# Sigmoid attention: the scores of four heads in one run, and their products with v in one run

## The chip, the cores and the metric

The kernel runs on one core of one Trainium2 chip. The metric is the device time of one execution, in microseconds (us). In the rows of the profile PE is TensorE (PEld its weight loads), ACT is ScalarE, DVE is VectorE, POOL is GpSimd and SP is SyncE, which issues the DMAs. A row of the timeline gives its start, its length, the engine, the line of the kernel, the operation, what it writes and reads, the shape, and how many instructions are merged in it; what stands in brackets is the time for which the engine was idle before it, and what ended that.

## What is computed

Attention with a sigmoid in place of the softmax, over 8 batches of 12 heads, 448 positions and 64 values a head, and then an MLP of 768 to 2048 to 768 with a sigmoid-approximated GELU over the 3584 tokens. All in float32.

```python
def _attn_ref(q, k, v):
    S = q.shape[2]
    scale = 1.0 / np.sqrt(q.shape[-1])
    scores = scale * np.matmul(q, k.transpose(0, 1, 3, 2)) - np.log(S)
    attn = 1.0 / (1.0 + np.exp(-scores))
    return np.matmul(attn, v).astype(np.float32)

def _moe_ref(x, w_in, w_out):
    h = x @ w_in
    g = h * (1.0 / (1.0 + np.exp(-1.702 * h)))
    return (g @ w_out).astype(np.float32)
```

Between the two, the heads of a position are put side by side into a row of x. The weights come as float64 words.

## The kernel before

**Pairs and chunks.** Two heads make a pair, 48 pairs in all; a pair's q and k, transposed, stand in one tile `qkraw` of 128 partitions (head 0 in 64 of them, head 1 in the other 64). The 448 keys are cut in three chunks of 128 and a left-over of 64. `split_pair` (line 541) splits q and k into a rounded part and a rest, both in a tile `qk`: the first on ACT or DVE (lines 442 and 443), the second on DVE (line 448). `scores` (line 567) makes the scores of one chunk for both heads in three terms, six matmuls; only the very first pair goes without a split. `scores_left` (line 585) makes the left-over scores of two pairs, four heads, at once, straight from `qkraw`. Each of these steps fills two banks of PSUM, and one `sigmoid` on ACT (line 560) empties them into an SBUF tile `a` (or `al` for the left-over). `values` (line 601) multiplies one chunk's `a` with v, and `values_left` (line 615) the left-over's; the products of both pairs of a unit of four heads are added up in one pair of banks, from which `to_x` (line 653) copies them into tiles of x, on ACT (line 658) or DVE (line 660), whichever the planner finds free. There are two copies per unit in the first and last batch, and four in the others, where a pair's rows fall in two blocks of x.

**Units.** Two pairs with one left-over are called a unit here: 24 of them. Before the change PE's order is: left-over scores of the unit; scores of its second pair; products of its first pair; scores of the next unit's first pair; products of this unit's second pair, with the left-over products at their end. So between a run of scores and the products that need its sigmoids another run always lies.

**Banks.** `two_banks` (line 555) gives the place numbers out: four pairs of banks, q0 to q3, place modulo 4. A step that writes a pair of banks waits for the readers of the step that had it before.

**The planner.** The kernel's instructions are put in order by a planner in the kernel's own text (`Plan.run`, line 106) before anything runs. PE's work comes as two lists of units, attention and MLP; a unit is begun when its tasks that are marked `alone` are ready, and is then issued whole, in its order. Work of ACT, DVE and SP goes by ready time and rank (`key`), the rank being that of the earliest PE step that needs it; `plan.early` sets the rank by hand for the copies to x and the loads of weights. On the chip each engine runs its list in that order and waits where it must. `BUFS` (line 27) tells how many tiles a ring has: a tile is written again when the readers of its last use are done.

**Beside attention.** The decoding of the weights from float64 (`decode`, line 460: sign, exponent and mantissa steps on DVE and ACT), the storing of decoded weights, and sums of weight blocks for the MLP run on DVE, ACT and SP while PE does attention. The MLP's first block (`first_block`, line 812) begins when the last attention unit is done; the other blocks follow in triples, with sums and differences of blocks in place of some products.

Of the kernel before, what the change touches and what calls it, by code (L numbers as in the profile page):

```python
# [24 lines left out]
WARM = 26  # L25

BUFS = dict(
    qk=2, vraw=3, a=5, al=1, raw64=2, e=4, qkraw=5, x32=8,
    pair=2, wsplit=4, q0=1, q1=1, q2=1, q3=1, h0=1, h1=1,
)  # L30
SLOTS = dict(s=1536, g=2048, t=384)
EARLY_SLOTS, LATE_SLOTS = dict(s=7, g=4, t=0), dict(s=0, g=9, t=13)
HORIZON, URGENT, SPARE, KEEP = 14, 4, 1, 2
AWAY = 3
AGAIN = ((1, 0), (1, 1))
BACKLOG, PRESSING = 6.0, 4

# [42 lines left out]
class Plan:  # L80
# [3 lines left out]
    def buffer(self, tag):  # L84
        b, ring = Buffer(), self.rings.setdefault(tag, [])
        b.turn = len(ring) % BUFS[tag]
        ring.append(b)
        return b
# [7 lines left out]
    def task(self, engine, cost, emit, deps=(), uses=()):  # L96
        return self.either({engine: cost}, {engine: emit}, deps, uses)
# [227 lines left out]
def sigmoid_attention_mlp(ctx: ExitStack, tc: tile.TileContext, qk, v, w, out):  # L325
# [11 lines left out]
    NC = S // P  # L337
# [38 lines left out]
    ps = spaces["q0"].tile([P, 512], F32, tag="q0_0", name="still", bufs=1)  # L376
# [9 lines left out]
    plan = Plan()  # L386
    task, either, buffer = plan.task, plan.either, plan.buffer
    def make(b, tag, shape, dtype, name):
        late = tag in LATE or tag == b.slot and int(tag[1:]) >= EARLY_SLOTS[tag[0]]
        if late and "late" not in spaces:  # L390
            att_stack.close()
            spaces["late"] = late_stack.enter_context(tc.tile_pool(name="late", bufs=2))
        if tag in ("h0", "h1") and tag not in spaces:
            for t in ("q1", "q0") if tag == "h0" else ("q3", "q2"):
                psum[t].close()
            banks(tag, "left" if tag == "h0" else "right")
        if late:
            pool = spaces["late"]
        else:
            pool = spaces.get(tag, sb)  # L400
        b.tile = pool.tile(shape, dtype, tag=tag if tag == b.slot else f"{tag}_{b.turn}", name=name, bufs=1)
        return b.tile
# [111 lines left out]
    x32, wrote, xs = {}, {}, {}  # L514
# [40 lines left out]
    def two_banks(place):  # L555
        b = buffer(f"q{place % 4}")
        b.tag = f"q{place % 4}"
        return b
# [8 lines left out]
    def scores(n, c, t_s, s, place):  # L567
        ps, a = two_banks(place), buffer("a")

        terms = ((0, 1), (1, 0), (0, 0)) if n else ((0, 0),)  # L570

        def emit():
            make(ps, ps.tag, [P, 2, 512], F32, f"sc{n}_{c}")
            src = [s.tile[:, 0], s.tile[:, 1]] if n else [s.tile]
            for i, (kk, qq) in enumerate(terms):
                for j, rows in enumerate(halves_of_rows):
                    nc.tensor.matmul(  # L577
                        ps.tile[:, j, :S], lhsT=src[kk][rows, S + c * P : S + (c + 1) * P], rhs=src[qq][rows, :S],
                        start=i == 0, stop=i == len(terms) - 1,
                    )  # L580

        t = task("PE", (0.7, 0.61, 0.61)[c] if n else 0.9, emit, t_s, [ps, s])
        return t, sigmoid(f"a{n}_{c}", a, ps, t), a

    def scores_left(n, sources, place):

        ps, a = two_banks(place), buffer("al")

        def emit():
            make(ps, ps.tag, [P, 2, 512], F32, f"sc{n}_{NC}")  # L590
            for cols, (_, src) in zip(halves_of_rows, sources):
                for j, rows in enumerate(halves_of_rows):
                    nc.tensor.matmul(  # L593
                        ps.tile[cols, j, :S], lhsT=src.tile[rows, S + NC * P :], rhs=src.tile[rows, :S],
                        start=True, stop=True, skip_group_check=True,
                    )

        t = task("PE", 0.8, emit, [t for ts, _ in sources for t in ts], [ps, *(b for _, b in sources)])
        return t, sigmoid(f"a{n}_{NC}", a, ps, t, "al"), a

    def values(n, c, t_a, a, t_v, vr, ps):

        def emit():
            if ps.tile is None:
                make(ps, ps.tag, [P, 2, 512], F32, f"av{n}")
            for j, cols in enumerate(halves_of_rows):
                at = ((n % 2 * 2 + j) * NC + c) * D
                nc.tensor.matmul(  # L608
                    ps.tile[cols, n % 2, :S], lhsT=vr.tile[:, at : at + D], rhs=a.tile[:, j],
                    start=c == 0, stop=False, skip_group_check=True,  # L610
                )

        return task("PE", (0.8, 0.75, 0.75)[c], emit, [t_a, t_v], [ps, a, vr])

    def values_left(t_a, a, t_v, vr, ps):

        def emit():
            for k, rows in enumerate(halves_of_rows):
                for j, cols in enumerate(halves_of_rows):
                    at = (4 * NC + j) * D  # L620
                    nc.tensor.matmul(  # L621
                        ps.tile[cols, k, :S], lhsT=vr.tile[rows, at : at + D], rhs=a.tile[rows, j],
                        start=False, stop=True, skip_group_check=True,
                    )

        return task("PE", 0.95, emit, [t_a, t_v], [ps, a, vr])
# [24 lines left out]
    copies = []  # L651

    def to_x(b, p, t, ps):
        bank = (b * NP + p) % 2
        for block, xb, first, into, cols in x32_places(b, p):
            n = cols.stop - cols.start
            copies.append(on_either(
                (0.2 + 0.00075 * n, lambda xb=xb, into=into, cols=cols: nc.scalar.copy(
                    xb.tile[:, into], ps.tile[:, bank, cols])),
                (0.15 + 0.00105 * n, lambda xb=xb, into=into, cols=cols: nc.vector.tensor_copy(  # L660
                    xb.tile[:, into], ps.tile[:, bank, cols])),
                [t], [xb, ps], first,
            ))
            wrote[block, p].append(copies[-1])
        split_x(b, p)
# [24 lines left out]
    firsts, urgent = [], []  # L690

    def attention():

        units, late, held_ = [], [], 0  # L700
        for n, (b, p) in enumerate(pairs):
            t_q, qkr, t_v, vr = load_pair(b, p)
            t_s, s = split_pair(b, p, t_q, qkr)
            firsts.append(t_s)
            left = scores_left(n, [first, (t_q, qkr)], held_ + 1) if n % 2 else None
            chunks = [scores(n, c, [t_s] if n else t_q[: c + 1], s, held_ + 1 + n % 2 + c) for c in range(NC)]
            run = [t for t, _, _ in chunks]
            if n % 2 == 0:
                first, chunks0, pair0 = (t_q, qkr), chunks, (b, p)
            else:  # L710

                units.append([left[0]])
                held_ += 1
                ps = two_banks(held_)
                both = [
                    [values(m, c, got[1], got[2], t_v, vr, ps) for c, got in enumerate(cs)]
                    for m, cs in ((n - 1, chunks0), (n, chunks))
                ]
                both[1].append(values_left(*left[1:], t_v, vr, ps))
                late.append(both[0])  # L720
                copied = len(copies)
                for pair in (pair0, (b, p)):
                    to_x(*pair, both[1][-1], ps)
                urgent.append(copies[copied:])
            if n > 2 and n % 2:

                plan.early += [(t, run[0]) for t in urgent[n // 2 - 1]]

            with_v = late.pop(0) if late else []
            for t in run[2:] + with_v:  # L730
                t.alone = False
            units.append(run + with_v)
            if n % 2:
                late.append(both[1])
        units.append(late.pop())
        place_of["next"] = held_ + 1
        return units

# [18 lines left out]
    def used_as(block):  # L757
        return [r for r, v in enumerate(W_USES) if v == block]
# [53 lines left out]
    def first_block():  # L812
# [5 lines left out]
        def pieces(m, h, i, got):  # L818
            out = []
            for k in range(2):  # L820
# [6 lines left out]
                count[0] += 1  # L827
                for r in used_as(2 * i + k) if (m, h) not in AGAIN else ():
                    save(m, r, h, slice(0, PIECE), into, b, t)
# [121 lines left out]
    def triple(one, blocks_before):  # L951
# [17 lines left out]
        def pieces_of(m, r):  # L969
            out = []  # L970
            for h in range(2):
                b, into, first = weights_ring(f"w{m}_{one}_{r}_{h}")
                ts = []
                if W_USES[r] < 8 and (m, h) in AGAIN:
                    i, k = divmod(W_USES[r], 2)
# [85 lines left out]
        class Net:  # L1061


            def __init__(self, m, defs, outs, uses, n, parts, name, finish):
# [18 lines left out]
                for v, cs in children.items():  # L1083
                    cs = sorted(cs, key=there)
                    for before, c in zip(cs, cs[1:]):
                        if c < len(PRODUCTS) and len(self.parents[c]) == 1:
                            away = there(c) - there(before)
                            if away >= AWAY:
                                self.seeds[c] = v
# [166 lines left out]
    main, nodes, ps = first_block()  # L1256
# [46 lines left out]
```

## Time and profile before

| what | time, us |
| --- | --- |
| median of 3 runs | 1060.55 (1060.08 to 1060.8) |
| the profiled execution | 1060.78 |
| its span, first to last instruction | 1059.0 |
| attention on PE, first scores to last left-over products | 3.93 to 261.2 |
| PE busy in the span | 1043.6 |
| DVE busy | 843.4 |
| ACT busy | 554.5 |
| longest wait of PE behind its warm-up (at 15.21, for DVE) | 2.00 |

The profiled execution lies 0.2 us over the median, and 1.8 us over its own span. Matmuls are pipelined, so their lengths overlap: how long a step holds PE is read from one start to the next, not from the length in the row. The granted clock of TensorE was 1.00 in all of the attention stage.

### The profile page before, as it was taken

To read this page: it belongs to the slowest core of one execution; us is meant where nothing else is said; L and a number is where in the kernel's file an instruction comes from. 1 tells how busy PE (TensorE), PEld (TensorE's weight loads), DVE (VectorE), ACT (ScalarE), POOL (GpSimd) and SP (SyncE) were. 2 spreads that over 40 slices of the span, in tenths; PEclk is the share of its full clock that TensorE was granted. 3 is DMA by queue.
4 is the path that set the end of the run, shared out by engine and by line. 5 is a ranking of instruction groups with operands and counts; after the bars stand their busy time and mean duration, and the time that the engine had idled before them with its cause. 6 is when DMAs were issued, how large, how long until landed. Compare 5 with 4: busy or idle time off the path is not lost.

```text
span 1059.0 us, 13676 instructions
## 1 busy us (share of the span) xinstructions
PE 1043.6 (99%) x5300; PEld 777.5 (73%) x5300; DVE 843.4 (80%) x770; ACT 554.5 (52%) x543; POOL 0.2 (0%) x4
## 2 busy tenths in 40 slices
PE   8999999999999999999999999999999999999997
PEld 4454545454788888888888788888888888788886
DVE  5988788873999856788898989999884596888684
ACT  7888788885655523434544444332443263534342
POOL 0000000000000000000000000000000000000000
PEclk9999999999999999999999999999999999999999
DMA  9899999883799997657656665869775545445765
GB/s 353 305 334 382 337 352 324 303 318 123 299 383 401 355 388 258 238 187 236 226 169 211 224 206 181 285 214 354 275 243 191 196 139 189 148 151 150 233 199 192
DMA packets 109104, 271.44 MB, mean 256 GB/s; under 512 B 8560, under 2 KB 69104, under 8 KB 106992
## 3 DMA queue, kind: packets, MB, share of 16 engines
q1 hardware_dynamic: 109040, 270.57, 73.1%
q8 instruction: 42, 0.69, 0.2%
q14 instruction: 22, 0.18, 0.1%
HBM read 185.60 MB, written 84.93 MB: 255 GB/s over the span
## 4 chain that ended last, share of the span: by engine, by line
PE 89%; DVE 4%; DMA 3%; ACT 2%; issue 1%; SPq 0%; ACTq 0%; DVEq 0%
PE p L800 54%; PE av L608 11%; PE sc L577 9%; PE h L800 6%; PE o_q L800 6%; PE av L621 2%; PE sc L593 2%; DMA qkraw<-qk 1%; DMA w<-c 1%; DMA w<-f 1%; DMA c<-wc 1%; DVE gp L1026 1%; ACT gp L1014 1%; DVE h L743 0%; ACT o L1156 0%
## 5 line engine op out<-in xcount | busy, mean ns | idle before, releaser
L800 PE MATMUL p<-gp,w 128*128 128x512 f32 x1440 | 329.5, 390 | 2.8 <-DVE gp L1026 1.2
L800 PE MATMUL p<-xp,w 128*128 128x512 f32 x1440 | 327.9, 389 | 1.0 <-DVE xp L1026 1.0
L800 PEld LDWEIGHTS p<-gp,w 128*128 128x128 f32 x1440 | 269.7, 188 | 61.3 <-DVE gp L1026 2.0
L800 PEld LDWEIGHTS p<-xp,w 128*128 128x128 f32 x1440 | 270.2, 188 | 57.5 <-DVE xp L1026 1.4
L563 ACT ACTIVATE a<-sc,bias 128x896 f32<-128x896 f32 x168 | 158.5, 1019 | 14.9 <-PE sc L577 10.9
L608 PE MATMUL av<-a,vraw 128*64 128x448 f32 x576 | 118.6, 547 | 0.0
L577 PEld LDWEIGHTS sc<-qk 64*128 64x128 f32 x846 | 75.8, 184 | 40.8 <-issue 14.0
L577 PE MATMUL sc<-qk 64*128 64x448 f32 x846 | 98.4, 373 | 2.6 <-DVE qk L448 2.0
L608 PEld LDWEIGHTS av<-a,vraw 128*64 128x64 f32 x576 | 37.1, 136 | 59.6 <-issue 56.4
L1026 DVE TENSOR_TENSOR gp<-h,gp 128x2048 fp32r<-128x2048 f32 x31 | 70.9, 2288 | 9.3 <-ACT gp L1014 8.9
L1156 ACT COPY h<-p 128x2048 f32<-128x2048 f32 x18 | 33.7, 1875 | 82.6 <-PE p L800 53.2
L800 PE MATMUL h<-x,w 128*128 128x512 f32 x288 | 66.6, 390 | 1.3 <-DVE x L660 1.3
L800 PE MATMUL o_q<-g,w 128*128 128x512 f32 x288 | 66.6, 389 | 1.2 <-ACT graw L856 1.2
L1190 DVE TENSOR_TENSOR h<-h,p 128x2048 f32<-128x2048 f32 x23 | 52.1, 2284 | 18.6 <-PE p L800 11.4
L1014 ACT CAST gp<-h 128x2048 fp32r<-128x2048 f32 x23 | 44.0, 1912 | 43.5 <-PE p L800 36.2
L800 PEld LDWEIGHTS h<-x,w 128*128 128x128 f32 x288 | 54.0, 188 | 13.3 <-DVE x L660 2.1
L800 PEld LDWEIGHTS o_q<-g,w 128*128 128x128 f32 x288 | 54.0, 188 | 12.8 <-ACT graw L856 1.6
L1156 ACT COPY o<-p 128x1536 f32<-128x1536 f32 x18 | 25.9, 1443 | 59.3 <-PE p L800 19.2
L448 DVE TENSOR_TENSOR qk<-qkraw,qk 128x896 fp32r<-128x896 f32 x47 | 51.2, 1089 | 6.4 <-ACT qk L442 5.9
L743 DVE TENSOR_TENSOR h<-h,h 128x2048 f32<-128x2048 f32 x24 | 54.7, 2285 | 0.1
L763 ACT CAST wc<-ws 128x384 fp32r<-128x384 f32 (+1 forms) x57 | 32.2, 580 | 42.2 <-DVE ws L743 26.8
L1014 ACT CAST xp<-x 128x1536 fp32r<-128x1536 f32 x19 | 28.1, 1480 | 39.4 <-PE p L800 32.3
(107 smaller groups left out, 975.0 us busy)
## 6 DMA issues: line engine op xcount, KB each, us to landing
w<-c SPq DMA_DIRECT2D x140, 384.0 KB, 4.4
w<-c SPq DMA_DIRECT2D x52, 768.0 KB, 4.6
w<-w SPq DMA_DIRECT2D x16, 1536.0 KB, 10.0
c<-wc SPq DMA_DIRECT2D x56, 384.0 KB, 5.4
qkraw<-qk SPq DMA_DIRECT2D x47, 448.0 KB, 6.5
vraw<-v SPq DMA_DIRECT2D x24, 448.0 KB, 4.9
xd<-x SPq DMA_DIRECT2D x42, 256.0 KB, 4.6
c<-wc SPq DMA_DIRECT2D x14, 768.0 KB, 7.2
```

The lines of the kernel that those rows point to most:

```text
L448: lambda: nc.vector.tensor_tensor(lo(), src(), hi().bitcast(F32), op=ALU.subtract),
L563: nc.scalar.activation(a.tile, ps.tile[:, :, :S], AF.Sigmoid, bias=bias, scale=scale)
L577: nc.tensor.matmul(ps.tile[:, j, :S], lhsT=src[kk][rows, S + c * P : S + (c + 1) * P], rhs=src[qq][rows, :S], start=i == 0, stop=i == len( ...
L593: nc.tensor.matmul(ps.tile[cols, j, :S], lhsT=src.tile[rows, S + NC * P :], rhs=src.tile[rows, :S], start=True, stop=True, skip_group_chec ...
L608: nc.tensor.matmul(ps.tile[cols, n % 2, :S], lhsT=vr.tile[:, at : at + D], rhs=a.tile[:, j], start=c == 0, stop=False, skip_group_check=True,)
L743: return task("DVE", cost, lambda: nc.vector.tensor_tensor(out(), x(), y(), op=op), deps, uses)
L763: t_hi = on_either((act(n), lambda: nc.scalar.copy(into()[:, 0], node.view())), (cast(n), lambda: nc.vector.tensor_copy(into()[:, 0], node ...
L800: nc.tensor.matmul(ps, lhsT=ws[:, a, c * P : (c + 1) * P], rhs=x[:, d, k], start=start and i == 0 and j == 0, stop=stop and i == len(todo) ...
L1014: t_hi = on_either((act(n), lambda: nc.scalar.copy(part(0)(), node.view())), (cast(n), lambda: nc.vector.tensor_copy(part(0)(), node.view())),
L1026: nc.vector.tensor_tensor(part(1)(), node.view(), part(0)().bitcast(F32), op=ALU.subtract)
L1156: t = on_either((act(self.n), lambda: nc.scalar.copy(view(), node.view())), (dve(self.n), lambda: nc.vector.tensor_copy(view(), node.view())),
L1190: nc.vector.tensor_tensor(view(), x.view(), y.view(), op=ALU.add if s0 == s else ALU.subtract)
```

## The change

PE's order in a unit becomes: left-over scores, six chunks of scores (first pair, then second), six chunks of products, left-over products. So the left-over products of one unit stand right ahead of the next unit's left-over scores. In the first unit the left-over scores come behind the first pair's. The whole of this is one unit for the planner, begun when its first four tasks (`LEADERS`) are ready. The place numbers follow: 1 for the left-over scores, 2 to 7 for the chunks (in the first unit 2 to 4 and 5 to 7 too), 8 for the products, and 8 further for each unit. The copies to x are ranked ahead of the next unit's first step, the left-over scores, where before it was the next unit's second-pair scores. The ring of `a` has six tiles in place of five, that of `qkraw` four in place of five; the two kinds have the same size.

```diff
 BUFS = dict(
-    qk=2, vraw=3, a=5, al=1, raw64=2, e=4, qkraw=5, x32=8,
+    qk=2, vraw=3, a=6, al=1, raw64=2, e=4, qkraw=4, x32=8,
...
+LEADERS = 4
...
-        units, late, held_ = [], [], 0
+        units, held_ = [], 0
         for n, (b, p) in enumerate(pairs):
             t_q, qkr, t_v, vr = load_pair(b, p)
             t_s, s = split_pair(b, p, t_q, qkr)
             firsts.append(t_s)
-            left = scores_left(n, [first, (t_q, qkr)], held_ + 1) if n % 2 else None
-            chunks = [scores(n, c, [t_s] if n else t_q[: c + 1], s, held_ + 1 + n % 2 + c) for c in range(NC)]
-            run = [t for t, _, _ in chunks]
+            if n % 2:
+                left = scores_left(n, [first, (t_q, qkr)], held_ + 1)
+            chunks = [scores(n, c, [t_s] if n else t_q[: c + 1], s, held_ + 2 + n % 2 * NC + c) for c in range(NC)]
             if n % 2 == 0:
                 first, chunks0, pair0 = (t_q, qkr), chunks, (b, p)
-            else:
-
-                units.append([left[0]])
-                held_ += 1
-                ps = two_banks(held_)
-                both = [
-                    [values(m, c, got[1], got[2], t_v, vr, ps) for c, got in enumerate(cs)]
-                    for m, cs in ((n - 1, chunks0), (n, chunks))
-                ]
-                both[1].append(values_left(*left[1:], t_v, vr, ps))
-                late.append(both[0])
-                copied = len(copies)
-                for pair in (pair0, (b, p)):
-                    to_x(*pair, both[1][-1], ps)
-                urgent.append(copies[copied:])
-            if n > 2 and n % 2:
-
-                plan.early += [(t, run[0]) for t in urgent[n // 2 - 1]]
-
-            with_v = late.pop(0) if late else []
-            for t in run[2:] + with_v:
+                continue
+            held_ += 8
+            ps = two_banks(held_)
+            both = [values(m, c, got[1], got[2], t_v, vr, ps)
+                    for m, cs in ((n - 1, chunks0), (n, chunks)) for c, got in enumerate(cs)]
+            both.append(values_left(*left[1:], t_v, vr, ps))
+            copied = len(copies)
+            for pair in (pair0, (b, p)):
+                to_x(*pair, both[-1], ps)
+            run = [t for t, _, _ in chunks0 + chunks]
+            plan.early += [(t, left[0]) for t in urgent]
+            urgent[:] = copies[copied:]
+            unit = [left[0], *run, *both] if n > 1 else [*run[:NC], left[0], *run[NC:], *both]
+            for t in unit[LEADERS:]:
                 t.alone = False
-            units.append(run + with_v)
-            if n % 2:
-                late.append(both[1])
-        units.append(late.pop())
+            units.append(unit)
```

## The prediction

> **What bounds the kernel now.** The page comes first: the busy time of each engine, and among the groups the sigmoid's.
>
> ```profile
> PE 1043.6 (99%) x5300; PEld 777.5 (73%) x5300; DVE 843.4 (80%) x770; ACT 554.5 (52%) x543; POOL 0.2 (0%) x4
> ...
> L563 ACT ACTIVATE a<-sc,bias 128x896 f32<-128x896 f32 x168 | 158.5, 1019 | 14.9 <-PE sc L577 10.9
> ```
>
> PE is busy nearly all the time, so a gain must come from matmul time or from one of its few waits. 168 sigmoids are 24 units of seven: six chunks (c0 to c5) and one left-over. ACT's 52% is a mean over the whole span; in the attention stage it is another figure. By windows (length, then busy time and instructions of PE, PEld, DVE, ACT and POOL, granted clock, DMA share, GB/s):
>
> ```profile
> 10.74:20.45 9.71, 7.71 (x53) 3.65 (x55) 6.44 (x7) 8.97 (x10) 0.00 (x0) 1.00 1.01 412
> 20.45:94.00 73.55, 73.55 (x536) 36.94 (x532) 63.27 (x74) 62.32 (x70) 0.00 (x0) 1.00 0.93 342
> 94.00:105.53 11.53, 10.88 (x81) 5.23 (x77) 10.87 (x13) 9.47 (x12) 0.00 (x0) 1.00 0.99 358
> 105.53:252.66 147.13, 147.13 (x1068) 73.84 (x1064) 116.80 (x141) 120.66 (x144) 0.00 (x0) 1.00 0.83 304
> ```
>
> These windows are cut at starts of left-over scores. ACT is busy 82 to 85% of the two long ones, PE 100%: ACT keeps up there, with little to spare. PE's own order in one unit, and at the end of the stage, where two runs of products happen to meet already:
>
> ```profile
> 221.14 0.93 PE L593 MATMUL sc<-qkraw 64*64 64x448 f32 x8
> 222.00 2.09 PE L577 MATMUL sc<-qk 64*128 64x448 f32 x18
> 224.02 2.48 PE L608 MATMUL av<-a,vraw 128*64 128x448 f32 x12
> 226.43 2.08 PE L577 MATMUL sc<-qk 64*128 64x448 f32 x18
> 228.44 2.48 PE L608 MATMUL av<-a,vraw 128*64 128x448 f32 x12
> 230.85 0.98 PE L621 MATMUL av<-a,vraw 64*64 64x448 f32 x8
> ...
> 242.16 0.93 PE L593 MATMUL sc<-qkraw 64*64 64x448 f32 x8
> ...
> 252.66 0.93 PE L593 MATMUL sc<-qkraw 64*64 64x448 f32 x8
> 253.53 2.09 PE L577 MATMUL sc<-qk 64*128 64x448 f32 x18
> 255.54 4.73 PE L608 MATMUL av<-a,vraw 128*64 128x448 f32 x24
> 260.20 0.98 PE L621 MATMUL av<-a,vraw 64*64 64x448 f32 x8
> ```
>
> From start to start: left-over scores 0.86, scores 2.02, products 2.41, scores 2.01, products 2.41, left-over products 0.80: a period of 10.51 (also 242.16 to 252.66).
>
> **What merging saves on PE.** Products: two runs apart take 2 x 2.41 = 4.82; the run of 24 takes 260.20 - 255.54 = 4.66, so 0.16 less. Scores: no two runs meet in this trace, but one run is cut by a wait:
>
> ```profile
> 94.00 0.93 PE L593 MATMUL sc<-qkraw 64*64 64x448 f32 x8
> 94.86 1.49 PE L577 MATMUL sc<-qk 64*128 64x448 f32 x12
> 96.97 0.89 PE L577 MATMUL sc<-qk 64*128 64x448 f32 x6 [0.62 <-ACT x L658]
> ```
>
> Two chunks last 1.49, three 2.09, so a chunk behind another costs 0.60, and a second run behind the first 1.80 in place of 2.01: 0.21 less (at worst, if the second run paid its own entry again, nothing). With the 0.16 the unit's floor on PE is 10.51 - 0.37 = 10.14. Were PE all that counts, 22 units would give back 8.1 us; without the scores' part the floor is 10.35, which the next part also passes, so the difference doesn't enter the sum.
>
> **What the new order puts in its place.** Before, three chunks of scores were followed by products of a run whose sigmoids lay a run back. Now seven PE steps in a row need a sigmoid each, on four pairs of banks. Counting places from the left-over scores as 1, c0 to c5 have 2 to 7 and the products 8. So c3 waits for the sigmoid of the left-over scores, c4 for that of c0, c5 for c1, and the products for c2 (place 4). That is four sigmoids in a row, the first of which stands behind the copies of the unit before. ACT's rows at one unit, at the first and last of the 22 that count, and at 94.00:
>
> ```profile
> 222.46 3.72 ACT L563 ACTIVATE a<-sc,bias 128x896 f32<-128x896 f32 x4
> ...
> 21.47 3.95 ACT L563 ACTIVATE a<-sc,bias 128x896 f32<-128x896 f32 x4 [0.25 <-PE sc L593]
> ...
> 243.50 3.71 ACT L563 ACTIVATE a<-sc,bias 128x896 f32<-128x896 f32 x4
> ...
> 96.33 0.59 ACT L658 COPY x<-av 128x128 f32<-128x128 f32 x2 [1.81 <-DVE x L660]
> 96.81 3.72 ACT L563 ACTIVATE a<-sc,bias 128x896 f32<-128x896 f32 x4
> ...
> 97.89 2.48 PE L608 MATMUL av<-a,vraw 128*64 128x448 f32 x12
> ```
>
> Four sigmoids in a row last 3.71, so they start 0.90 apart, against 0.60 for a chunk of scores. At 94.00 one sees what a late one does: the first sigmoid ends at 96.81 + 1.02 = 97.83 and the products, whose banks it frees, start 0.06 later; so about 0.05 from ACT's end to PE. Let s be the time from a left-over scores' start to the first sigmoid's: 1.02 at 20.45, 1.32 at 221.14, 1.34 at 242.16, 2.81 at 94.00. Read in this way over the 22 units from 20.45 to 242.16 its mean is 1.43 (1.36 without the one at 94.00). The copies make it so long: four of them, on ACT and DVE in turn, wait for one another (17.0 and 31.3 us of such waits in the stage), and nothing in the change touches that.
>
> ```profile
> DVE x L660 <- ACT x L658: 31.3, 24, 7.7
> ACT x L658 <- DVE x L660: 17.0, 22, 1.8
> ```
>
> So the products start at s + 3.71 + 0.05 (c5 can start at s + 1.80 + 1.02 + 0.05, and from a chunk that starts after a wait to the products it took at most 97.89 - 96.97 = 0.92: s + 3.79, about the same), and the new period is s + 3.76 + 4.66 + 0.80 = **s + 9.22**, never below 10.14. At 1.43 it is 10.65: 0.14 longer than now. What is queued behind the wait is PE's own: twelve pairs of products, then the next left-over scores; ACT waits for those, so the delay passes on in full. c3 to c5 have their sigmoids by s + 3.71 + 2.70 = 7.84, and c5's products start some 3.9 behind the first, at 9.1: no wait there. ACT then has about 3 us until the next copies for a sign (1.6) and a cast (0.95).
>
> By the Trainium skill (TensorEngine Tiling (Array Packing), Performance Considerations, PSUM Bottleneck) array tiles speed up TensorE but not the emptying of PSUM, which can become the bottleneck. That speaks against this change, and the 0.90 beside 0.60 bears it out; by PE's rows alone the sum below would be 11 us lower.
>
> **The sum, against the profiled execution's 1060.78.**
> 1. Start.
>
> ```profile
> 7.81 0.98 PE L593 MATMUL sc<-qkraw 64*64 64x448 f32 x8
> 8.72 2.09 PE L577 MATMUL sc<-qk 64*128 64x448 f32 x18
> 10.74 2.48 PE L608 MATMUL av<-a,vraw 128*64 128x448 f32 x12
> 15.21 2.09 PE L577 MATMUL sc<-qk 64*128 64x448 f32 x18 [2.00 <-DVE qk L448]
> ...
> 20.45 0.93 PE L593 MATMUL sc<-qkraw 64*64 64x448 f32 x8
> ...
> 7.18 5.66 ACT L563 ACTIVATE a<-sc,bias 128x896 f32<-128x896 f32 x6 [0.33 <-PE sc L577]
> ...
> 16.72 1.09 DVE L448 TENSOR_TENSOR qk<-qkraw,qk 128x896 fp32r<-128x896 f32 x1
> ```
>
> The 2.00 wait for the third pair's split goes: the products of the first unit stand there. But c3 now needs the left-over sigmoid, third of the six, 8.98 to 9.99: c3 at 10.04, products at 12.06, left-over products 16.72, next left-over scores at 17.52 in place of 20.45: -2.93. The splits of unit 2 end by 17.81, ahead of their use at 18.4 and 20.2.
>
> 2. The 22 units: 22 x 10.65 = 234.2 against 252.66 - 20.45 = 232.2: +2.0.
> 3. The last unit now holds both runs of scores: s is 1.00 there (sigmoid at 253.66), products at 4.76, left-over products at 9.42 in place of 7.54: +1.88.
>
> ```profile
> 253.66 1.91 ACT L563 ACTIVATE a<-sc,bias 128x896 f32<-128x896 f32 x2 [0.22 <-PE sc L593]
> ```
>
> Sum: -2.93 + 2.0 + 1.9 = **+0.95, that is 1061.7 for a profiled execution and 1061.5 beside the median of 1060.55**.
>
> Edits that I cost at nothing. Six `a` buffers in place of five: seven sigmoids waited 1.7 us for one (row below), on ACT, with PE busy beside them; with six, one per chunk, that goes, and ACT's order behind copies stays. Four `qkraw` in place of five: a pair's load is now issued when the left-over scores of its buffer's last unit are done, and lands in 6.5 us, while its split is due over 10 us later; if SP were late by more than that, the split would be late in full. `vraw` loads and the spills hang on left-over products and copies as before. The splits of both pairs wait for the end of c2 and c5, some 5 us ahead of use, for 1.7 us of DVE each; without that cover each would add its lateness. The earlier rank of the copies changes nothing while they are the first work ready. `LEADERS` matters only to what the planner would put ahead of a unit, and the MLP's first unit needs the bank that the last copies free. Behind the stage the planner orders anew what PE runs without gaps; I take 0, and +-3 us as an estimate of mine from its waits there, of which the longest is 1.3 (last row below), one or two gone or added.
>
> ```profile
>   PE av L608: 1.7, 7
> ...
> qkraw<-qk SPq DMA_DIRECT2D x47, 448.0 KB, 6.5
> ...
> PE h L800 <- DVE x L660: 1.3, 1, 1.3
> ```
>
> **Rivals.** *The copies get out of the way* (faster). Where DVE or ACT does them without the exchange, s is 1.02, as at 20.45: a period of 10.24, 22 x 0.31 = 6.9 less than now, with start and end 1052.6. From s = 1.29 on average the sum is past -0.2%. Against it: the copies' code and their ranks are the same; for it: the planner deals them out anew.
>
> *Copies or sigmoids later* (slower). Now PE hides an s of up to 1.81 (its first products stand 2.88 behind the left-over scores and need one sigmoid, s + 1.07); with the change each 0.1 of it is 2.2 us over the stage. The place is DVE: at 94.00 ACT waited 1.81 for its copy and s was 1.45 above the others' mean, and DVE is 86% busy up to there. The sum passes +0.2% at a mean s of 1.48, 0.05 above now's. One such delay more in every third unit gives 7 x 1.45 = 10: 1072; in every sixth, 1067.
>
> *The clock falls with the small waits.* PE would wait up to 0.6 us per unit. A half clock for one unit would cost 10 us, for all some 220: 1280. Against it: the granted clock stayed 1.00 in 94.00:105.53, with two PE gaps that sum to 0.65, and in 10.74:20.45, with 2.00. The Trainium skill (TensorE: Matmul & The Clock Gate, A second HAM failure mode: psum-queue depth-cycling) tells of such a loss where PE idles shortly and often; those windows speak against it here.
>
> *The order isn't what the text says*: units are kept whole by the planner once begun, so I give it no share.
>
> **Chances.** Forecast (ACT paces, gain and loss cancel) 0.41, its own range 1058.5 to 1062.6; faster rival 0.28; slower one 0.30; clock 0.01. About 0.2% (2.1 us) is what a measurement of this kernel can tell from none. So faster 0.28, same 0.41, slower 0.31. The range takes in most of both rivals: 1053.5 to 1067.
>
> **What would show it.** Right: score runs of 36 and product runs of 24 matmuls; PE waits ahead of the first products of a unit, put down to ACT's sigmoid; periods of about s + 9.22; second unit at 17.5. Wrong: periods of 10.14 without a wait (then s is below 0.92 or the banks come free otherwise), or waits put down to DVE splits or to DMA.

## The result, and the profile after

The changed kernel takes 1062.99 us (median of 19 runs, 1060.38 to 1065.23) where the kernel before, run beside it, takes 1060.58: a ratio of 1.0019, with a 95% interval of 1.0011 to 1.0027. So it is slower by about 0.2%, at the edge of what I had called no change; the forecast was 1061.5. The profiled execution took 1064.14, with a span of 1062.4.

The page of the changed kernel, the lines that answer to those of before:

```profile
PE 1044.8 (98%) x5300; PEld 777.5 (73%) x5300; DVE 847.2 (80%) x779; ACT 548.9 (52%) x534; POOL 0.2 (0%) x4
...
L564 ACT ACTIVATE a<-sc,bias 128x896 f32<-128x896 f32 x168 | 153.7, 1030 | 0.7 <-PE sc L594 0.6
```

PE is busy as before, by the page. What ACT waited for ahead of its sigmoids has shrunk from 14.9 us to 0.7: its sigmoids no longer wait for PE, so PE must be waiting for them. PE's timeline, at the start (with ACT's rows there), in a usual unit and at the end of the stage:

```profile
3.93 2.85 PE L578 MATMUL sc<-qkraw 64*128 64x448 f32 x12
6.71 0.98 PE L594 MATMUL sc<-qkraw 64*64 64x448 f32 x8
9.08 2.11 PE L578 MATMUL sc<-qk 64*128 64x448 f32 x18 [1.39 <-ACT a L564]
11.12 4.73 PE L609 MATMUL av<-a,vraw 128*64 128x448 f32 x24
...
6.28 0.94 ACT L443 CAST qk<-qkraw 128x896 fp32r<-128x896 f32 x1 [4.06 <-DMA qkraw<-qk]
7.13 6.39 ACT L564 ACTIVATE a<-sc,bias 128x896 f32<-128x896 f32 x7
...
16.59 0.93 PE L594 MATMUL sc<-qkraw 64*64 64x448 f32 x8
...
211.31 0.93 PE L594 MATMUL sc<-qkraw 64*64 64x448 f32 x8
212.17 4.25 PE L578 MATMUL sc<-qk 64*128 64x448 f32 x36
216.44 4.73 PE L609 MATMUL av<-a,vraw 128*64 128x448 f32 x24
221.10 0.98 PE L622 MATMUL av<-a,vraw 64*64 64x448 f32 x8
221.91 0.93 PE L594 MATMUL sc<-qkraw 64*64 64x448 f32 x8
...
253.88 0.93 PE L594 MATMUL sc<-qkraw 64*64 64x448 f32 x8
...
263.35 0.98 PE L622 MATMUL av<-a,vraw 64*64 64x448 f32 x8
```

The runs are merged as the text of the change says: 36 matmuls of scores, 24 of products. The products last 4.66 from start to start. The scores, however, take 4.27 to the products and not 3.82, and the waits within them are so short that the timeline merges over them. The period is 10.60 there, against 10.51 before. ACT at the same unit:

```profile
212.19 0.59 ACT L659 COPY x<-av 128x64 f32<-128x64 f32 x2 [1.35 <-issue]
212.67 6.41 ACT L564 ACTIVATE a<-sc,bias 128x896 f32<-128x896 f32 x7
```

And in the second unit, at 16.59, the copies of the first:

```profile
16.83 0.62 DVE L661 COPY x<-av 128x448 f32<-128x448 f32 x1 [1.89 <-PE av L622]
17.49 0.54 ACT L659 COPY x<-av 128x448 f32<-128x448 f32 x1 [1.84 <-DVE x L661]
```

DVE has the first copy and ACT the second, so s is 1.34 there. At the same place of the kernel before, 20.45, ACT's copy came first, at 20.69, and s was 1.02: the planner dealt the copies out otherwise.

Here is who waited for ACT's sigmoids in the stage, from the view of the waits (us in total, times, longest), before and after:

```profile
PEld sc L577 <- ACT a L563: 12.7, 18, 0.7
PEld av L608 <- ACT a L563: 3.2, 10, 0.4
```

```profile
PEld av L609 <- ACT a L564: 20.3, 71, 0.4
...
PEld sc L578 <- ACT a L564: 14.9, 38, 2.2
```

The weight loads of scores and products now wait for a sigmoid 109 times, in place of 28. In the unit shown all seven sigmoids run in one go, from 1.36 behind the left-over scores' start. Here s is 1.36, and the period less s is 9.24. So it is in each of the 22 units from 16.59 to 253.88: period less s lies between 9.22 and 9.24, while s itself goes from 1.09 to 4.11.

Where the time went, from the two spans (1059.0 and 1062.4), each step by the starts of the rows shown here and in the prediction:

| step | forecast | measured |
| --- | --- | --- |
| start, to the second unit's left-over scores (20.45, now 16.59) | -2.93 | -3.86 |
| 22 units (232.2, now 237.3) | +2.0 | +5.1 |
| last unit, to its left-over products (7.54, now 9.47) | +1.88 | +1.93 |
| behind it, to the end (798.80, now 799.05) | 0 | +0.25 |
| sum | +0.95 | +3.4 |

The largest single piece of the 22 units is one with s = 4.11, from 79.74 to 93.08. DVE, ACT and PE there, by the timeline:

```profile
74.27 0.96 DVE L444 CAST x<-x 128x1536 fp32r<-128x1536 f32 x1 [2.07 <-DMA x<-xd]
...
78.48 1.16 DVE L444 CAST qk<-qkraw 128x896 fp32r<-128x896 f32 x2
79.55 2.09 DVE L449 TENSOR_TENSOR qk<-qkraw,qk 128x896 fp32r<-128x896 f32 x2
...
82.42 0.29 DVE L661 COPY x<-av 128x128 f32<-128x128 f32 x1
82.75 0.42 ACT L659 COPY x<-av 128x320 f32<-128x320 f32 x1 [3.10 <-DVE x L661]
...
83.85 5.50 ACT L564 ACTIVATE a<-sc,bias 128x896 f32<-128x896 f32 x6
84.01 3.58 PE L578 MATMUL sc<-qk 64*128 64x448 f32 x24 [1.73 <-ACT x L659]
```

DVE stood for 2.07 us at a cast of x, for the MLP much later, whose load had not landed. All that was queued behind it on DVE, the splits and then the first copy, came late, ACT waited 3.10 us for that copy, and the sigmoids behind it started at 83.85.

DVE's rows of the kernel before show such a wait too, ahead of its unit at 94.00:

```profile
89.39 0.96 DVE L443 CAST x<-x 128x1536 fp32r<-128x1536 f32 x1 [1.32 <-DMA x<-xd]
...
95.81 0.48 DVE L660 COPY x<-av 128x320 f32<-128x320 f32 x1
```

DVE stood there for 1.32 us at another cast of the same x, and from 89.39 on it was busy without a gap up to the copy at 95.81, the one for which ACT waited 1.81 us.

### The profile page after: what moved, and what is told of

It reads as the page before. It is cut to its first block, busy times and chain, and to the rows that moved or that the text cites. A ratio compares the mean times of both kernels' runs of the same rounds, so it can differ in the third digit from the quotient of the medians.

```text
span 1062.4 us, 13688 instructions
## 1 busy us (share of the span) xinstructions
PE 1044.8 (98%) x5300; PEld 777.5 (73%) x5300; DVE 847.2 (80%) x779; ACT 548.9 (52%) x534; POOL 0.2 (0%) x4
## 4 chain that ended last, share of the span: by engine, by line
PE 91%; DVE 3%; DMA 3%; ACT 2%; issue 1%; SPq 0%; ACTq 0%; DVEq 0%
PE p L791 57%; PE av L609 10%; PE sc L578 8%; PE h L791 6%; PE o_q L791 6%; PE av L622 2%; PE sc L594 1%; DMA xd<-x 1%; DMA x<-xd 1%; ACT gp L1005 1%; DVE gp L1017 0%; DMA qkraw<-qk 0%; ACT o L1147 0%; DMA w<-c 0%; DMA w<-f 0%
## 5 line engine op out<-in xcount | busy, mean ns | idle before, releaser
L564 ACT ACTIVATE a<-sc,bias 128x896 f32<-128x896 f32 x168 | 153.7, 1030 | 0.7 <-PE sc L594 0.6
L609 PE MATMUL av<-a,vraw 128*64 128x448 f32 x576 | 113.5, 543 | 0.5
L578 PE MATMUL sc<-qk 64*128 64x448 f32 x846 | 101.1, 377 | 4.0 <-ACT x L659 1.7
L661 DVE COPY x<-av 128x128 f32<-128x128 f32 (+6 forms) x44 | 17.0, 399 | 40.5 <-ACT x L659 28.0
```

The lines of the kernel that those rows point to most:

```text
L564: nc.scalar.activation(a.tile, ps.tile[:, :, :S], AF.Sigmoid, bias=bias, scale=scale)
L578: nc.tensor.matmul(ps.tile[:, j, :S], lhsT=src[kk][rows, S + c * P : S + (c + 1) * P], rhs=src[qq][rows, :S], start=i == 0, stop=i == len( ...
L609: nc.tensor.matmul(ps.tile[cols, n % 2, :S], lhsT=vr.tile[:, at : at + D], rhs=a.tile[:, j], start=c == 0, stop=False, skip_group_check=True,)
```

## The experiments

Two theories stood at the outset. **A**: ACT's sigmoids pace the unit, the period is s + 9.22, and s is set by copies that go between ACT and DVE in turn. **B**: the merging gains nothing, or the loss comes from something else that was changed, as the smaller ring of q and k. "New" is the changed kernel's order, "old" that of the kernel before. Each ratio is to the kernel before, run on the same chip beside it. In the table, s is its mean over the 22 units, and the third column the time from the second unit's left-over scores to the last unit's, both from the one profiled execution; the last column is the forecast's 1061.5 with that s in place of 1.43: 1061.5 + 22 x (s - 1.43).

| run | s | 22 units | median, us | ratio (interval) | by s |
| --- | --- | --- | --- | --- | --- |
| the changed kernel | 1.56 | 237.3 | 1062.99 | 1.0019 (1.0011 to 1.0027) | 1064.4 |
| new_copies_dve | 1.28 | 231.1 | 1058.25 | 0.9985 (0.9976 to 0.9994) | 1058.2 |
| old_copies_dve | 1.03 | 231.1 | 1060.66 | 1.0005 (0.9996 to 1.0015) | |
| new_idle_ahead | 2.13 | 249.7 | 1077.51 | 1.0164 (1.0151 to 1.0177) | 1076.9 |
| old_idle_ahead | 2.07 | 238.4 | 1066.87 | 1.0069 (1.0056 to 1.0082) | |
| new_half_sigmoid | 1.56 | 225.6 | 1052.23 | 0.9917 (0.9904 to 0.9930) | |
| old_half_sigmoid | 1.42 | 231.9 | 1060.80 | 0.9994 (0.9982 to 1.0006) | |
| new_late_x_plan | 1.45 | 234.9 | 1061.89 | 1.0006 (0.9998 to 1.0015) | 1061.9 |
| new_dve_late_x | 1.16 | 228.4 | 1055.05 | 0.9946 (0.9934 to 0.9958) | 1055.6 |
| new_act_late_x | 1.18 | 229.5 | 1056.37 | 0.9958 (0.9946 to 0.9969) | 1056.0 |
| old_dve_late_x | 1.03 | 231.1 | 1060.79 | 0.9999 (0.9990 to 1.0008) | |
| new_old_rings | 1.45 | 234.8 | 1061.94 | 1.0011 (1.0002 to 1.0019) | 1061.9 |
| new_one_handover | 1.31 | 232.4 | 1058.56 | 0.9975 (0.9966 to 0.9984) | 1058.9 |

**The cost of a late sigmoid: new_idle_ahead and old_idle_ahead.** Two idle copies on ACT ahead of each left-over sigmoid; the planner isn't told, so the order of the rest stays.

```diff
+    idle = const.tile([P, 256], F32, name="idle")
+    nc.vector.memset(idle, 0.0)
...
             make(a, tag, [P, 2, S], F32, name)
+            if tag == "al":
+                for _ in range(2):
+                    nc.scalar.copy(idle, idle)
             nc.scalar.activation(a.tile, ps.tile[:, :, :S], AF.Sigmoid, bias=bias, scale=scale)
```

> The new order with two idle copies of 256 columns on ACT ahead of each left-over sigmoid, unknown to the planner, so that the order of all engines stays: s grows by about 0.6. Theory A: it passes on in full, 22 x 0.6 = 13 us: 1076, ratio about 1.014. Rival B: hidden beside other waits, ratio 1.002 to 1.005.

> The order before with the same two idle copies. Theory A: s + 0.6 over 1.81 only in the units with a long s; by the values of s read from the trace before that sums to 3 to 5 us: 1064 to 1066, ratio 1.003 to 1.005, less than half of what the new order loses. Rival B: the same loss in both orders.

PE's timeline of the new order with the idle copies, then of the old one:

```profile
199.83 0.93 PE L600 MATMUL sc<-qkraw 64*64 64x448 f32 x8
200.69 4.88 PE L584 MATMUL sc<-qk 64*128 64x448 f32 x36
205.60 4.73 PE L615 MATMUL av<-a,vraw 128*64 128x448 f32 x24
...
211.07 0.93 PE L600 MATMUL sc<-qkraw 64*64 64x448 f32 x8
```

```profile
203.54 0.93 PE L599 MATMUL sc<-qkraw 64*64 64x448 f32 x8
204.40 2.09 PE L583 MATMUL sc<-qk 64*128 64x448 f32 x18
206.94 2.48 PE L614 MATMUL av<-a,vraw 128*64 128x448 f32 x12 [0.45 <-ACT a L569]
```

The new order loses 14.5 us by its median against the changed kernel (12.4 of them in the 22 units), where 13 were expected; the old one 6.9 against the kernel before, where 3 to 5 were expected. In the new order the idle copies stand on the path at the start as well (the second unit begins at 18.41, in place of 16.59). The old order's mean s rose to 2.07, past the 1.81 that it hides, and PE waits for the sigmoid ahead of its products (0.45 at 206.94). Summed over the units, its s passes 1.81 by 7.3 us, that of the kernel before by 1.0; the difference, 6.3, is near the 6.2 by which its 22 units grew. So the miss was in s and not in the 1.81. Both orders have the same wait, but the old one has it only from an s of 1.81, the new one from the start. B's "hidden" and "the same loss in both" are out.

**What the merged runs save: new_half_sigmoid and old_half_sigmoid.** Both kernels leave out the sigmoid of the second half of each tile, and all products read the first half, so a sigmoid takes ACT 0.64 us on average in place of 1.03; the planner goes on reckoning with the old cost.

```diff
-            nc.scalar.activation(a.tile, ps.tile[:, :, :S], AF.Sigmoid, bias=bias, scale=scale)
+            nc.scalar.activation(a.tile[:, 0], ps.tile[:, 0, :S], AF.Sigmoid, bias=bias, scale=scale)
...
-                    ps.tile[cols, n % 2, :S], lhsT=vr.tile[:, at : at + D], rhs=a.tile[:, j],
+                    ps.tile[cols, n % 2, :S], lhsT=vr.tile[:, at : at + D], rhs=a.tile[:, 0],
...
-                        ps.tile[cols, k, :S], lhsT=vr.tile[rows, at : at + D], rhs=a.tile[rows, j],
+                        ps.tile[cols, k, :S], lhsT=vr.tile[rows, at : at + D], rhs=a.tile[rows, 0],
```

> The new order with ACT's cost of a sigmoid about halved: only the first head of each pair gets its sigmoid, and the products of both heads use it. The planner's costs, and so all orders, stay. Theory A (PE saves 0.37 a unit by the merged runs, ACT's sigmoids take it back): the first products no longer wait, every period falls to PE's floor of 10.14 (the unit in which the copies come late keeps some 1.3 more); 22 units 224 to 225 in place of 237; 1050 to 1052, ratio 0.990 to 0.992. Rival D (merged runs save nothing, or not on scores): periods of 10.35 to 10.5, ratio 0.995 to 0.999.

> The order before with the same halved sigmoid, the control. Theory A: PE's own run-by-run order sets 10.51, ACT was hidden; ratio 0.998 to 1.001. Rival: ACT held the old order too, and it gains as much as the new one.

PE's timeline of the new order:

```profile
201.81 0.93 PE L594 MATMUL sc<-qkraw 64*64 64x448 f32 x8
202.67 3.91 PE L578 MATMUL sc<-qk 64*128 64x448 f32 x36
206.51 4.73 PE L609 MATMUL av<-a,vraw 128*64 128x448 f32 x24
...
211.97 0.93 PE L594 MATMUL sc<-qkraw 64*64 64x448 f32 x8
```

36 matmuls of scores take 3.84 from their start to the products', where twice 2.02 were needed; the period is 10.16, and the whole 1052.23. The 22 units take 225.6, a little over the 224 to 225 expected, as two of them last 10.86 and 11.34 and the expectation allowed for one. The same cut in ACT's work does nothing for the old order (0.9994). So the merging does save what the forecast said, 0.35 a unit, and ACT takes it back.

**What makes s long: the copies.** All of them on DVE, in both orders (in new_act_late_x below all on ACT, with `nc.scalar.copy`):

```diff
-            copies.append(on_either(
-                (0.2 + 0.00075 * n, lambda xb=xb, into=into, cols=cols: nc.scalar.copy(
-                    xb.tile[:, into], ps.tile[:, bank, cols])),
-                (0.15 + 0.00105 * n, lambda xb=xb, into=into, cols=cols: nc.vector.tensor_copy(
-                    xb.tile[:, into], ps.tile[:, bank, cols])),
-                [t], [xb, ps], first,
-            ))
+            def copy(xb=xb, into=into, cols=cols, first=first):
+                first()
+                nc.vector.tensor_copy(xb.tile[:, into], ps.tile[:, bank, cols])
+
+            copies.append(task("DVE", 0.15 + 0.00105 * n, copy, [t], [xb, ps]))
```

> The new order with all copies to x on DVE. Theory A (ACT paces the unit, period = s + 9.22, s set by the copies that go between ACT and DVE in turn): ACT is free for the first sigmoid, s falls from 1.56 on average to 1.0 to 1.1, periods 10.2 to 10.35, 22 units about 226 to 228 us in place of 237; total 1053 to 1056, ratio to before 0.993 to 0.996. Rival B (the loss comes from something else that the change did, the smaller ring of q and k or DMA, and the copies are hidden): 1062 to 1064, ratio 1.002. Rival C (DVE, which gets some 10 us more work in the stage, becomes late): s falls in most units but a few units stall by 1 to 3 us, ratio 0.997 to 1.003.

> The order before with all copies to x on DVE, the control. Theory A: the old order hides an s up to 1.81, so the same edit is worth nothing here: ratio 0.999 to 1.001, at best the 1.0 us stall at 94.00 goes. Rival B': if the copies on DVE are a gain by themselves (less ACT work in all), this one gains as much as the new order does.

The timeline of new_copies_dve, ACT and PE in a usual unit, then ACT where a unit stalls:

```profile
103.98 6.40 ACT L564 ACTIVATE a<-sc,bias 128x896 f32<-128x896 f32 x7 [0.96 <-PE sc L594]
...
102.89 0.93 PE L594 MATMUL sc<-qkraw 64*64 64x448 f32 x8
...
113.20 0.93 PE L594 MATMUL sc<-qkraw 64*64 64x448 f32 x8
...
71.68 1.47 ACT L443 CAST x<-x 128x1536 fp32r<-128x1536 f32 x1 [3.37 <-DMA x<-xd]
```

ACT now waits for the left-over scores themselves: s is 1.09 in 18 of the 22 units (1.06 in one more), and the period 10.31. The old order gains nothing. But the ratio, 0.9985, misses the expected 0.993 to 0.996: in one unit s is 4.29, as ACT, which now had the cast of x, stood 3.37 us for its load; in two more it is 1.63, with an exponent step of 1.5 us on ACT ahead of the sigmoids. The ratio is the one that rival C gave, but not by its cause: I had looked for a DVE with too much work; it was ACT that stood, and for the same load as DVE in the changed kernel.

**That stall: new_late_x_plan and new_dve_late_x.** The planner is told that the loads of block 0's x take 4 us longer, so that it puts their readers later:

```diff
         t = [dma(lambda j=j: x.tile[:, 1, j].bitcast(F32), lambda j=j: spill[block][k][:, j], P * T * 4 / 1024,
                  [spilled[block, k * NJ + j]], [x], first) for j in range(NJ)]
+        for load in t:
+            load.landing += 4.0
```

> The new order where the planner reckons 4 us more for the loads of block 0's x, so that DVE or ACT no longer stands waiting for them ahead of a unit's splits and copies. Theory A: the unit with s = 4.1 (79.74) falls back to the others' 1.3 to 1.7, which is worth about 2.5 us: 1060 to 1061, ratio 0.9995 to 1.0005, and P - s stays 9.22. Rival E (the stall only moves to another unit, as DVE has the same work): ratio 1.001 to 1.003.

> Both edits: all copies on DVE, and 4 us more reckoned for the loads of x. Theory A: s 1.09 in nearly all units, periods 10.31, 22 units 227 to 228.5 in place of 231; 1054 to 1056, ratio 0.995 to 0.997, faster than both kernels. Rival E: another unit takes the stall, ratio 0.998 to 0.999 as with the copies alone.

In new_late_x_plan nothing in the stage waits for that load any more; the worst unit, from 80.10, is 11.23 long in place of 13.34, with an s of 2.01 in place of 4.11, and the 22 units take 2.4 us less. The medians, 1061.89 and 1062.99, differ by less, and the ratio of 1.0006 lies just past what was expected; its interval reaches into rival E's 1.001 to 1.003, so it is the trace that speaks against E. With the copies on DVE too the kernel takes **1055.05, a ratio of 0.9946 (0.9934 to 0.9958)**: faster than both, and a little more so than the 0.995 expected at best. PE's timeline there:

```profile
204.12 0.93 PE L594 MATMUL sc<-qkraw 64*64 64x448 f32 x8
204.98 3.96 PE L578 MATMUL sc<-qk 64*128 64x448 f32 x36
208.96 4.73 PE L609 MATMUL av<-a,vraw 128*64 128x448 f32 x24
...
214.42 0.93 PE L594 MATMUL sc<-qkraw 64*64 64x448 f32 x8
```

**Is it the exchange, or the copies' own time? new_act_late_x and new_one_handover; and the controls old_dve_late_x and new_old_rings.** In new_one_handover the first pair's copies are on ACT, and the second pair's, made to follow them, on DVE; both have the later x. new_old_rings is the changed kernel with `a=5` and `qkraw=5`.

> The new order with all copies on ACT, and 4 us more reckoned for the loads of x. Theory A with its second half (what makes s long is the exchange between ACT and DVE, not the copies' work itself): ACT's own copies follow one another some 0.1 to 0.45 us apart, so s is about 1.25 to 1.35 with four copies and 1.15 with two, although ACT now does all of them; periods 10.4 to 10.55; between new_late_x_plan and new_dve_late_x, ratio 0.997 to 0.999. Rival F (each engine's copies cost their own time, so all of them on ACT is the worst case): s of 1.7 and more, ratio 1.002 to 1.006.

> The new order, the first pair's copies on ACT and then the second pair's on DVE, and 4 us more reckoned for the loads of x: the same sharing of work between ACT and DVE as in the changed kernel, but one handover per unit in place of up to three, and ACT done first. Theory A, second half (what makes s long is that ACT has a copy behind one of DVE's): s is at the floor of about 1.09 that the left-over scores' own end sets, though the work is shared; 22 units 227 to 229.5, ratio 0.994 to 0.996. Rival G (sharing itself costs, by both engines reading the same banks): s 1.3 to 1.6 as in the changed kernel, ratio 0.999 to 1.001.

> The order before with both edits of new_dve_late_x. Theory A: worth at most the 1.0 us stall: ratio 0.998 to 1.001, so the 5 us of new_dve_late_x belong to the new order. Rival: the edits help any order, 0.995 to 0.997.

> The new order with the rings of before, five tiles of the sigmoids' output and five of q and k. Theory A: c5's sigmoid writes the tile that c0's products of the same unit read, free at s + 4.6, ahead of its turn at s + 5.4: nothing on the path, and q and k come 10 us ahead with either ring; ratio 1.001 to 1.003 as the changed kernel, P - s 9.22. Rival B (the smaller ring of q and k costs the new order time): 0.995 to 1.000.

ACT's timeline of new_act_late_x:

```profile
173.14 1.09 ACT L660 COPY x<-av 128x320 f32<-128x320 f32 x4
174.09 6.43 ACT L564 ACTIVATE a<-sc,bias 128x896 f32<-128x896 f32 x7
```

With four copies, all on ACT, s is 1.20; its mean over the 22 units is 1.18, where the sharing of the same copies makes it 1.45 (new_late_x_plan). Four copies in a row take ACT 1.09 us; it was the waits between them that cost. The ratio, 0.9958, is better than I had expected. Rival F is out.

ACT's timeline of new_one_handover, a usual unit and one of five with a longer s:

```profile
133.22 0.59 ACT L663 COPY x<-av 128x192 f32<-128x192 f32 x2 [0.70 <-PE av L622]
134.06 2.81 ACT L564 ACTIVATE a<-sc,bias 128x896 f32<-128x896 f32 x3 [0.24 <-PE sc L594]
...
143.53 0.59 ACT L663 COPY x<-av 128x256 f32<-128x256 f32 x2 [1.51 <-PE av L622]
144.20 1.48 ACT L495 ACTIVATE expo<-expo 128x1536 uint16<-128x1536 uint16 x1
145.59 1.89 ACT L564 ACTIVATE a<-sc,bias 128x896 f32<-128x896 f32 x2
```

Sharing with one handover costs next to nothing: s is at most 1.09 in 17 of 22 units, and in two units PE waits for a copy of DVE's, 0.30 and 0.18 us. Rival G's 1.3 to 1.6 in all units is out. Yet the run misses its expected 0.994 to 0.996 (0.9975), as in four of the other five ACT has an exponent step of 1.5 us between the copies and the first sigmoid, as at 144.20 (in the fifth it stands ahead of the copies). So the handover was not all of it: whatever stands on ACT at that place makes s longer, and s is paid in full. Why the planner put it there in this variant and not in the others I didn't follow up.

old_dve_late_x, 0.9999, says that both edits gain nothing in the old order: the 5.9 us by which the new order with them is ahead of the kernel before (1060.97 to 1055.05 in new_dve_late_x) need the new order. new_old_rings, 1.0011, can't be told from the changed kernel's 1.0019, as the intervals overlap. Its period less s is 9.22 to 9.24 as well, so the rings have no part in that. In its profile, though, no cast waits for a load of x, the worst s is 2.30 in place of 4.11, and the 22 units take 2.5 us less. That the new rings have no part in the stall, through the planner's order, is thus not shown.

## Why the prediction was right, and what it had too small

- **The saving of merged runs** (0.37 a unit, a floor of 10.14): 10.16 with ACT's load cut. The score part, for which no row of before had two runs in one, was right: 0.19 (2.02 + 2.01 less 3.84), with 0.21 forecast.
- **The period of s + 9.22**: 9.22 to 9.24 in all 22 units, and from 9.20 to 9.27 in nearly all units of the new order's other runs with whole sigmoids (new_one_handover has two at 9.5 and 9.7). Of the rows that gave it, those of the step from a sigmoid's end to PE came from the one unit at 94.00, where the old order had been caught by the same kind of wait.
- **The term of the 22 units was mis-sized**, +2.0 where +5.1 was measured, and in it only s: the forecast took the mean of before, 1.43, as "nothing in the change touches that", and 1.56 was measured. That step failed, in two parts of about the same size. The unit with the stall has 4.11 where before it had 2.81: 0.06 of the mean. The other 21 have 1.44 on average (34.31 - 4.11 = 30.20, over 21) where the others before had 1.36: the rest, 0.07. For these the planner dealt the copies out anew, as the forecast itself said it might (16.83 and 17.49 above). For the stall, the forecast read DVE's lateness at 94.00 as its load of work; the rows at 89.39 and 74.27 show in both kernels a wait for a load of x, which holds the engine that has the cast, DVE here and ACT in new_copies_dve. In the changed kernel new_late_x_plan shows by experiment that it is worth 2.1 us of s; for the unit at 94.00 only the trace says it (1.32 of the 1.45 us by which its s stood out).
- **The start** came out 0.93 better, -3.86. From c3 on it went as forecast (7.51 us to the next left-over scores, with 7.48 forecast). But c3 stands behind the second of ACT's sigmoids, and the forecast had taken the third, from ACT's order in the kernel before. The second ends at about 7.13 + 0.90 + 1.01 = 9.04, and c3 starts at 9.08; in new_idle_ahead the idle copies, which stand right ahead of the left-over sigmoid, follow the first one too (at 9.11), and c3 comes at 10.90. The very first scores were faster as well: 2.78 to the left-over ones in this execution, 3.88 in that of before (last section). It took both. By an estimate from the same rows the order alone would have given some 0.2 (the left-over scores would have ended at 7.81 + 0.98 = 8.79, and the forecast had their sigmoid at 8.98), the faster scores alone less than 0.1 (the third sigmoid at 7.13 + 1.80 = 8.93). Without the faster scores some 0.2 would have been left, so most of the 0.93 is luck, and it hid about a third of what the 22 units cost more than forecast.
- **The last unit and what lies behind** were as forecast (+1.93 for +1.88; +0.25 for 0 +-3).
- **The rivals.** "The copies get out of the way" didn't happen by itself, but when it was made to happen it gave 1055.05, with 1052.6 reckoned for an s of 1.02. Its turning point, s = 1.29 for -0.2%, fits roughly: new_copies_dve has 1.28 and 0.9985. "Copies or sigmoids later" is where the changed kernel went: its s of 1.56 lies past the 1.48 where the forecast put that rival's edge, its ratio at the edge itself, and its median 0.4 us past the forecast's own range, which ended at 1062.6. The granted clock read 1.00 in the 22 units of the changed kernel, and 0.999 over the whole of it, though PE waited in every unit: the clock rival is out.

The table's last column shows that one number carries the rest: with s from each profile, 1061.5 + 22 x (s - 1.43) comes within 0.7 us of seven medians, 1055 to 1078. Some of that closeness is luck, as the second unit begins anywhere from 16.45 to 18.41 in these seven profiles, with 17.52 in the forecast. For the changed kernel it gives 1064.4, near the profiled execution's 1064.14, and above its median. That the stall is longer or shorter from one execution to the next would explain this, and the spread of 4.9 us; the clock doesn't explain the spread, as the lowest and the highest run both have 0.999. But only one execution was profiled, and the kernel before spreads over 3.9 us and new_old_rings over 4.1, so it stays open.

## What to carry to other kernels

Merging runs of like matmuls saves their entries, but with a fixed number of PSUM buffers it also takes away the distance between a run and the engine that empties it: find the chain that frees the buffer of the first step behind the long run, and set its length beside the run's. What the old order hid (here a first sigmoid that starts up to 1.81 us behind the left-over scores) is then paid in full, unit by unit; so look at once at the work that stands ahead of that chain, and at whether two engines wait for each other in it. An engine that runs in order should not be given a reader of a DMA before it has landed when something urgent is queued behind.

## What the runs showed of the hardware

The very first scores, twelve float32 matmuls from 3.93 on, took from 2.5 to 3.9 us up to the left-over scores in the fourteen profiles, in either order (3.88 in the kernel before, 2.78 in the changed one, 2.48 in old_dve_late_x). They start in pairs: in the kernel before the steps from pair to pair are 0.91, 0.75, 0.75, 0.63 and 0.38 us, in the changed one 0.81 and then 0.38, and in old_dve_late_x 0.50 and then 0.38. The granted clock of that stretch reads 1.00 in both of the first two. So the clock row doesn't show what slowed them, which stays open, and the starts of two profiles can differ by 1.4 us over the same twelve matmuls.
